# Top-k attention before a mixture of experts: pairs of heads with operands transposed on the host, v stationary

## The chip, the core and the metric

The kernel runs on one core of one Trainium2 chip. Time is device microseconds (us) of one launch. What the host does to the inputs ahead of the launch is not part of it. The engines that matter are TensorE (matmuls and transposes, shown as PE; its weight loads as PEld), VectorE (DVE), ScalarE (ACT), GpSimd (POOL) and the queue that issues most DMAs (SP).

## What is computed

Inputs q, k, v are (8, 8, 576, 64) in float32: 8 batches, 8 heads, 576 positions, 64 numbers a head. Per batch and head:

```
scores = q @ k.T / 8
kth    = 32nd largest of each row of scores
attn   = softmax(where(scores >= kth, scores, -1e9))
out    = attn @ v
```

The heads' outputs side by side make 4608 tokens of 512 numbers. Then a mixture of experts with 8 experts, each token going to one of them:

```
logits = x @ w_gate                    # (4608, 8)
e      = argmax(logits)                # one expert a token
gate   = softmax(logits)[e]
y      = gate * (relu(x @ w1[e]) @ w2[e])     # 512 -> 1024 -> 512
```

## The kernel before

Attention goes by pairs of batches p (four), and in a pair head by head (eight), so there are 32 units. The two batches' 2 x 576 queries of a head make nine tiles of 128 rows: four of the first batch, four of the second, and a ninth with both tails of 64. That is 288 tiles of 128 queries by 576 keys.

`load_head` brings q, k and v of a head with nine DMAs on SP, two heads ahead. `prep_head` turns q and k into qT and kT on TensorE (eight transposes of 128x128, two of 64 rows), with the first batch's 64 numbers on rows 0 to 63 and the second's on rows 64 to 127; ScalarE copies them from PSUM.

A tile then goes through three steps. `scores` (L183) multiplies one 64-row half of qT with kT, 512 keys and then 64, and ScalarE copies the 576 scores to s. `weights` (L194) finds the 32 largest on VectorE in four rounds of MAX8 with three MATCH_REPLACE between them; after the first round ScalarE makes nbias (L203) and the exponential ex (L204); then one instruction (L212) compares s with the 32nd value, multiplies by ex and sums the row into z. VectorE adds a small number to z and takes its reciprocal rz. `values` (L223) transposes the weights on TensorE into pm (four blocks) and pt (the last 64 keys), ScalarE copies them to wm and wt, and five products with wm and wt stationary and 64 columns of v streaming give 128 queries by 64 numbers; ScalarE scales them by rz into the token buffer x (L241). The result shares the PSUM buffer of pt, of which there is one.

The loop (L333) emits for tile n: the scores of tile n+1, the weights of tile n, the values of tile n-1. The order in which instructions stand on each engine is not that of the text: a planner orders them by when their operands and buffers should be ready; each engine then takes its own list in order. Buffers: two for scores in PSUM, three for s, two for ex and scr, three for w.

When a pair of batches is through, `route` (L243) computes the logits in nine rounds (four transposes into PSUM, a copy to xT, four products), the expert of each token and its place in that expert's list. GpSimd scatters the token ids to the lists with nine indirect DMAs, each of which waits for the one before; x goes to DRAM. A routing's logits share the one PSUM buffer of pt, its transposes the one of `prep_head`.

After the last routing, a table says which expert and which piece of its list each of 25 blocks of 256 tokens has. For each block, the expert's weights (4 MB) are loaded two blocks ahead, tokens are gathered, transposed, and put through both layers (L410, L417), and the rows are scattered to the output.

Of the kernel before, what the change touches and what calls it, by code (L numbers as in the profile page):

```python
# [30 lines left out]
def kernel(  # L31
    ctx: ExitStack,
    tc: tile.TileContext,
    q: bass.AP,
    k: bass.AP,
    v: bass.AP,
# [16 lines left out]
    B, H, S, D = q.shape  # L53
# [3 lines left out]
    P = 128  # L57
    NC = 4
    SM = NC * P
    ST = S - SM  # L60
    NT = 2 * NC + 1
# [9 lines left out]
    assert D == 64 and ST == 64 and Dm == H * D and N == B * S and B % 2 == 0  # L71
# [5 lines left out]
    wpool = ctx.enter_context(tc.tile_pool(name="wpool", bufs=3))  # L77
# [28 lines left out]
    for p in range(NP):  # L106
        t = const.tile([P, NT], I32, name=f"tok_id{p}")
        b0 = 2 * p * S
        nc.gpsimd.iota(t[:, 0:NC], pattern=[[1, NC]], base=b0, channel_multiplier=NC)
        nc.gpsimd.iota(t[:, NC:2 * NC], pattern=[[1, NC]], base=b0 + S, channel_multiplier=NC)  # L110
# [7 lines left out]
    def load_w(e):  # L118
        w1 = wpool.tile([P, 1, DT, F], F32, name="w1")
        nc.sync.dma_start(w1, w1v[:, bass.ds(e, 1), :, :])  # L120
        w2 = wpool.tile([P, 1, FT, Dm], F32, name="w2")
        nc.sync.dma_start(w2, w2v[:, bass.ds(e, 1), :, :])
        return w1, w2

    cnt = None
    first_w = None

    with (
        tc.tile_pool(name="pad", bufs=1) as padp,
        tc.tile_pool(name="load", bufs=2) as load,  # L130
        tc.tile_pool(name="att", bufs=2) as att,
        tc.tile_pool(name="xp", bufs=2) as xp,
# [5 lines left out]
        loaded, ready = {}, {}  # L138

        def load_head(p, h):  # L140
            got = []
            for nm, src in (("q", q), ("k", k), ("v", v)):
                if nm == "v":
                    m = load.tile([P, 2, NC, D], F32, name="v_m", bufs=3)
                    nc.sync.dma_start(
                        m, src[2 * p:2 * p + 2, h, 0:SM, :].rearrange("b (p c) d -> p b c d", c=NC)
                    )
                else:
                    m = load.tile([P, NC, 2, D], F32, name=nm + "_m", bufs=3)
                    for b in range(2):  # L150
                        nc.sync.dma_start(
                            m[:, :, b, :], src[2 * p + b, h, 0:SM, :].rearrange("(p c) d -> p c d", c=NC)
                        )
                t = load.tile([ST, 2, D], F32, name=nm + "_t", bufs=3)
                nc.sync.dma_start(t, src[2 * p:2 * p + 2, h, SM:S, :].rearrange("b p d -> p b d"))
                got.append((m, t))
            loaded[p, h] = got

        def prep_head(p, h):
            (qm, qt), (km, kt), vv = loaded.pop((p, h))  # L160
            xT = []
            for nm, m in (("qT", qm), ("kT", km)):
                o = att.tile([P, S], F32, name=nm)
                ps = ps_1.tile([P, SM], F32, name="tr")
                for c in range(NC):
                    nc.tensor.transpose(ps[:, c * P:(c + 1) * P], m[:, c, :, :], ident)
                nc.scalar.copy(o[:, 0:SM], ps)
                xT.append(o)
            ps = ps_1.tile([P, SM], F32, name="tr")
            for n, t in enumerate((qt, kt)):  # L170
                nc.tensor.transpose(ps[:, n * ST:(n + 1) * ST], t, ident[0:ST, 0:ST])
            for n in range(2):
                nc.scalar.copy(xT[n][:, SM:S], ps[:, n * ST:(n + 1) * ST])
            ready[p, h] = (xT[0], xT[1], vv)

        def parts(i):
            """(batch of the pair, rows of the tile, columns of its queries)"""
            if i < 2 * NC:
                b, c = divmod(i, NC)
                return [(b, slice(0, P), slice(c * P, (c + 1) * P))]  # L180
            return [(b, slice(b * ST, (b + 1) * ST), slice(SM, S)) for b in range(2)]

        def scores(p, h, i):  # L183
            qT, kT, _ = ready[p, h]
            ps = ps_s.tile([P, S], F32, name="sc")
# [4 lines left out]
            s = att.tile([P, S], F32, name="s", bufs=3)  # L190
            nc.scalar.copy(s, ps)  # L191
            return s

        def weights(s):  # L194
# [16 lines left out]
            z = small.tile([P, 1], F32, name="z")  # L211
            nc.vector.scalar_tensor_tensor(  # L212
                out=w, in0=s, scalar=tops[:, TOP_K // 8 - 1, 7:8], in1=ex,
                op0=ALU.is_ge, op1=ALU.mult, accum_out=z,
            )
            rz = small.tile([P, 1], F32, name="rz", bufs=4)
            nc.vector.tensor_scalar_add(z, z, EPS)
            nc.vector.reciprocal(rz, z)
            return w, rz

        xt = {}

        def values(p, h, i, w, rz):  # L223
            _, _, (vm, vt) = ready[p, h]
            if h == 0 and i == 0:
                xt[p] = xp.tile([P, NT, XW], F32, name="x")
            pm = ps_w.tile([P, NC, P], F32, name="wT")
            pt = ps_1.tile([P, 512], F32, name="po")
# [3 lines left out]
            wm = att.tile([P, NC, P], F32, name="wm")  # L232
            wt = att.tile([ST, P], F32, name="wt")
            nc.scalar.copy(wm, pm)  # L234
            nc.scalar.copy(wt, pt[0:ST, 0:P])  # L235
            po = pt[:, P:P + D]
            for b, rows, _ in parts(i):
                for c in range(NC):
                    nc.tensor.matmul(po[rows, :], wm[:, c, rows], vm[:, b, c, :], start=(c == 0), stop=False)  # L239
                nc.tensor.matmul(po[rows, :], wt[:, rows], vt[:, b, :], start=False, stop=True)  # L240
            nc.scalar.activation(xt[p][:, i, h * D:(h + 1) * D], po, AF.Copy, scale=rz)  # L241

        def route(p):  # L243
# [4 lines left out]
            for i in range(NT):  # L248
                ps = ps_1.tile([P, DT, P], F32, name="xtr", tag="tr")
# [55 lines left out]
            for b in range(2):  # L305
                r0 = (2 * p + b) * S
                nc.sync.dma_start(
                    x_rows[r0:r0 + SM, :].rearrange("(p c) w -> p c w", c=NC), x[:, b * NC:(b + 1) * NC, :]
# [3 lines left out]
        heads = [(p, h) for p in range(NP) for h in range(H)]  # L312
        work = [(p, h, i) for p, h in heads for i in range(NT)]
        load_head(*heads[0])
        load_head(*heads[1])
        prep_head(*heads[0])

# [7 lines left out]
        def finish(n, wr):  # L325
            p, h, i = work[n]
            values(p, h, i, *wr)
            if h == H - 1 and i == NT - 1:
                route(p)

        s_next = scores(*work[0])
        wr_prev = None
        for n, (p, h, i) in enumerate(work):  # L333
            hn = p * H + h
            if i == 0 and hn + 2 < len(heads):
                load_head(*heads[hn + 2])
            if i == NC and hn + 1 < len(heads):
                prep_head(*heads[hn + 1])
            if i == 0 and hn == 3:
                first_w = load_w(0)  # L340
            s = s_next
            if n + 1 < len(work):
                s_next = scores(*work[n + 1])
            wr = weights(s)
            if wr_prev is not None:
                finish(n - 1, wr_prev)
            wr_prev = wr
        finish(len(work) - 1, wr_prev)
# [23 lines left out]
    with (  # L372
        tc.tile_pool(name="mlp", bufs=2) as mlp,
# [6 lines left out]
        def load_slot(j):  # L380
# [5 lines left out]
            else:  # L386
                w = load_w(nc.sync.value_load(slot_i[0:1, 0, j:j + 1], min_val=0, max_val=E - 1))
# [71 lines left out]
```

## Time and profile before

| | |
|---|---|
| three runs | 2889.40, 2894.57, 2893.51 us; median 2893.51 |
| profiled execution, span from first to last instruction | 2891.7 us; no other time of that execution is given |
| TensorE busy | 2733.2 us (95%) |
| VectorE busy | 1743.3 us (60%) |
| ScalarE busy | 858.8 us (30%) |
| GpSimd busy | 138.4 us (5%) |

A profile row of a group gives line, engine, operation, output and inputs by the program's names, their shapes, the count, then busy time in us and the mean duration of one in ns, then the engine's idle time ahead of them and what ended it. A timeline row gives start and duration in us. Instructions of one engine overlap a little, so the distance from start to start, not the duration, is what one costs in a row of them. A float32 product has two records on TensorE.

### The profile page before, as it was taken

What the parts mean: (1) busy time and instruction counts of PE and PEld (TensorE: products, weight loads), DVE (VectorE), ACT (ScalarE), POOL (GpSimd) and SP (SyncE); (2) the same over time, 40 slices, a digit from 0 to 9 for tenths busy, and PEclk for the clock granted to TensorE, in tenths of its full rate; (3) what the DMA queues carried; (4) which work ended last, traced back from release to release, by engine and by line L of the source; (5) the groups of instructions that cost most, each with busy time, mean ns of one, the idle gap of its engine ahead of it and who ended that gap; (6) DMA issues with size and microseconds to landing.
All of it is one profiled execution on the core that took longest, in us unless ns stands there. A gap on an engine that the chain in (4) does not pass through costs nothing. (4 is left out here: it accounts for less than half of the span.)

```text
span 2891.7 us, 27400 instructions
## 1 busy us (share of the span) xinstructions
PE 2733.2 (95%) x9288; PEld 1798.0 (62%) x9288; DVE 1743.3 (60%) x4280; ACT 858.8 (30%) x2097; POOL 138.4 (5%) x165
## 2 busy tenths in 40 slices
PE   8999999999999989999999899999829999999999
PEld 5666666666666666666666566666626666666665
DVE  7888888588888857888885788889410101010100
ACT  3343343233333333333333333433300111111010
POOL 0000000000000000000000100000011111111110
PEclk9999999999999999999999999999999999999999
DMA  4000000100000010000000200000045545455540
GB/s 126 13 17 13 13 17 5 54 16 13 17 13 13 9 49 15 19 13 13 17 9 5 57 13 9 5 5 1 1 169 178 183 171 181 167 183 177 173 156 4
DMA packets 144669, 167.19 MB, mean 58 GB/s; under 512 B 90764, under 2 KB 99084, under 8 KB 143506
## 3 DMA queue, kind: packets, MB, share of 16 engines
q1 hardware_dynamic: 135378, 142.84, 15.7%
q0 software_dynamic: 9152, 22.60, 2.0%
q8 instruction: 74, 1.21, 0.2%
q14 instruction: 65, 0.53, 0.1%
HBM read 146.34 MB, written 22.73 MB: 58 GB/s over the span
## 5 line engine op out<-in xcount | busy, mean ns | idle before, releaser
L189 PE MATMUL sc<-kT,qT 64*128 64x64 f32 (+3 forms) x1280 | 802.1, 765 | 0.0
L239 PEld LDWEIGHTS po<-v_m,wm 128*128 128x128 f32 (+1 forms) x2560 | 515.1, 306 | 349.8 <-ACT ex L204 327.3
L201 DVE MAX8 tops<-scr 128x8 f32<-128x576 f32 x864 | 622.8, 748 | 0.0
L239 PE MATMUL po<-v_m,wm 128*128 128x64 f32 (+1 forms) x2560 | 573.6, 406 | 5.0 <-ACT wt L235 4.8
L206 DVE MATCH_REPLACE8 scr<-tops,scr 128x576 f32<-128x576 f32 x576 | 426.8, 743 | 0.0
L189 PEld LDWEIGHTS sc<-kT,qT 64*128 64x128 f32 (+1 forms) x1280 | 290.2, 293 | 190.0 <-issue 153.2
L201 DVE MAX8 tops<-s 128x8 f32<-128x576 f32 x288 | 218.0, 757 | 309.0 <-ACT s L191 307.3
L410 PE MATMUL ph<-xTs,w 128*128 128x256 f32 x1600 | 353.0, 381 | 14.1 <-DVE xTs L405 14.1
L417 PE MATMUL py<-w,hT 128*128 128x512 f32 x800 | 347.4, 592 | 0.0
L241 ACT ACTIVATE x<-po,rz 128x64 f32<-128x64 f32 x288 | 90.7, 315 | 861.5 <-PE po L240 722.1
L410 PEld LDWEIGHTS ph<-xTs,w 128*128 128x128 f32 x1600 | 302.8, 191 | 60.1 <-DVE xTs L405 19.8
L230 PE MATMUL wT<-ident,w 128*128 128x128 f32 x1152 | 319.7, 430 | 0.0
L421 DVE TENSOR_SCALAR y<-py,xg 128x512 f32<-128x512 f32 x50 | 37.6, 751 | 447.4 <-PE py L417 447.4
L413 ACT ACTIVATE hT<-ph 128x256 f32<-128x256 f32 x200 | 76.8, 384 | 696.4 <-PE ph L410 637.7
L417 PEld LDWEIGHTS py<-w,hT 128*128 128x128 f32 x800 | 152.0, 190 | 180.7 <-issue 179.4
L212 DVE SCALAR_TENSOR_TENSOR w<-s,tops,ex 128x576 f32<-128x576 f32 x288 | 231.7, 805 | 13.6 <-PE po L231 9.2
L230 PEld LDWEIGHTS wT<-ident,w 128*128 128x128 f32 x1152 | 213.2, 219 | 28.3
L204 ACT ACTIVATE ex<-s,nbias 128x576 f32<-128x576 f32 x288 | 223.0, 774 | 8.4
L234 ACT COPY wm<-wT 128x512 f32<-128x512 f32 x288 | 168.8, 586 | 175.5 <-PE wT L230 166.9
L206 DVE MATCH_REPLACE8 scr<-tops,s 128x576 f32<-128x576 f32 x288 | 213.9, 743 | 0.0
L240 PE MATMUL po<-v_t,wt 64*128 64x64 f32 (+1 forms) x640 | 206.0, 424 | 0.0
L191 ACT COPY s<-sc 128x576 f32<-128x576 f32 x288 | 182.0, 632 | 6.3 <-PE sc L189 3.9
(92 smaller groups left out, 1313.2 us busy)
## 6 DMA issues: line engine op xcount, KB each, us to landing
w<-in_moe_w_dram SPq DMA_DIRECT2D x50, 2048.0 KB, 9.9
x_rows<-x SPq DMA_DIRECT2D x8, 1026.0 KB, 6.1
q_m<-in_q_dram SPq DMA_DIRECT2D x64, 128.0 KB, 2.6
k_m<-in_k_dram SPq DMA_DIRECT2D x64, 128.0 KB, 2.5
v_m<-in_v_dram SPq DMA_DIRECT2D x32, 256.0 KB, 2.9
x_rows<-x SPq DMA_DIRECT2D x8, 128.2 KB, 5.5
q_t<-in_q_dram SPq DMA_DIRECT2D x32, 32.0 KB, 2.2
k_t<-in_k_dram SPq DMA_DIRECT2D x32, 32.0 KB
```

The lines of the kernel that those rows point to most:

```text
L189: nc.tensor.matmul(ps[rows, c0:c1], qT[d, cols], kT[d, c0:c1], start=True, stop=True)
L191: nc.scalar.copy(s, ps)
L201: nc.vector.max(out=tops[:, r, :], in_=src)
L204: nc.scalar.activation(ex, s, AF.Exp, scale=scale, bias=nbias)
L206: nc.vector.match_replace(out=scr, in_to_replace=tops[:, r, :], in_values=src, imm_value=NEG)
L212: nc.vector.scalar_tensor_tensor(out=w, in0=s, scalar=tops[:, TOP_K // 8 - 1, 7:8], in1=ex, op0=ALU.is_ge, op1=ALU.mult, accum_out=z,)
L230: nc.tensor.transpose(pm[:, c, :], w[:, c * P:(c + 1) * P], ident)
L234: nc.scalar.copy(wm, pm)
L239: nc.tensor.matmul(po[rows, :], wm[:, c, rows], vm[:, b, c, :], start=(c == 0), stop=False)
L240: nc.tensor.matmul(po[rows, :], wt[:, rows], vt[:, b, :], start=False, stop=True)
L410: nc.tensor.matmul(ph, w1[:, 0, dt, f * P:(f + 1) * P], xT[:, dt, :], start=(dt == 0), stop=(dt == DT - 1))
L417: nc.tensor.matmul(py, hT[:, f, c * P:(c + 1) * P], w2[:, 0, f, :], start=(f == 0), stop=(f == FT - 1))
```

## The change

Attention now goes batch by batch and by pairs of heads: (b, u) with u from 0 to 3, 32 units as before. q and k come from the host as (8, 512, 576), already transposed, so that two heads lie on the two 64-row halves of a 128-row slice; v comes as (8, 576, 512). `load_head` and `prep_head` are gone; `load_qk` loads two units at a time, `load_v` a whole batch.

A unit's nine tiles are four of the first head, four of the second, and the ninth with both heads' last 64 queries. `scores` takes a pair of tiles, one of each head on the same queries, and emits their products alternately, each as two times 288 keys; a score tile has two PSUM banks. `weights` makes nbias on GpSimd and leaves z as one column of a unit's (128, 9). `transposed` copies the transposed weights of all nine tiles into one large buffer wT (and wTt for the last 64 keys). `outputs`, once a unit, multiplies with v stationary (64 columns of a head) and the weights streaming, 288 queries at a time, the two heads into the two halves of one PSUM tile; copies the result to oT; transposes it back; and multiplies by the reciprocals on VectorE on the way into x. Routing's transposes share the PSUM buffer of the weights' tail, its logits that of the outputs. There are four buffers for s. The experts' weight pool is opened after attention; the first expert's weights have a pool of their own and are asked for in the fifth unit (before, the fourth). The numbering of tokens in tiles, and with it the row stores, changes.

```diff
+        def load_qk(b, u):
+            qb = load.tile([P, 2, S], F32, name="qb")
+            nc.sync.dma_start(qb, qt[b, u * P:(u + 2) * P, :].rearrange("(u p) s -> p u s", p=P))
...
-            for b, rows, cols in parts(i):
-                d = slice(b * D, (b + 1) * D)
-                for c0, c1 in ((0, SM), (SM, S)):
-                    nc.tensor.matmul(ps[rows, c0:c1], qT[d, cols], kT[d, c0:c1], start=True, stop=True)
+            for i in tiles:
+                ps = ps_s.tile([P, 2, SM], F32, name="sc")
+                todo += [(ps, h, rows, cols) for h, rows, cols in parts(i)]
+                got.append(ps)
+            for j in range(2):
+                for ps, h, rows, cols in todo:
+                    d = slice(h * D, (h + 1) * D)
+                    nc.tensor.matmul(
+                        ps[rows, j, 0:HF], qu[d, cols], ku[d, j * HF:(j + 1) * HF], start=True, stop=True
+                    )
+            out_s = []
+            for ps in got:
+                s = att.tile([P, 2, HF], F32, name="s", bufs=4)
+                nc.scalar.copy(s, ps[:, :, 0:HF])
...
-                    nc.scalar.mul(nbias, tops[:, 0, 0:1], -scale)
+                    nc.gpsimd.tensor_scalar(nbias, tops[:, 0, 0:1], -scale, None, ALU.mult)
...
-            nc.vector.tensor_scalar_add(z, z, EPS)
-            nc.vector.reciprocal(rz, z)
...
+        def transposed(b, u, i, w):
+            wT, wTt, _ = units[b, u]
+            pm = ps_w.tile([P, NC, P], F32, name="wTm")
+            pt = ps_1.tile([P, SM], F32, name="wTl")
             for c in range(NC):
                 nc.tensor.transpose(pm[:, c, :], w[:, c * P:(c + 1) * P], ident)
             nc.tensor.transpose(pt[0:ST, 0:P], w[:, SM:S], ident)
...
+                nc.scalar.copy(wT[:, :, h, q], pm)
+                nc.scalar.copy(wTt[:, h, q], pt[0:ST, 0:P])
...
+        def outputs(b, u):
+            vb = vs_of[b]
+            wT, wTt, z = units[b, u]
+            rz = small.tile([P, NT + 1], F32, name="rz", bufs=2)
+            nc.vector.tensor_scalar_add(rz[:, 0:NT], z, EPS)
+            nc.vector.reciprocal(rz[:, 0:NT], rz[:, 0:NT])
+            nc.vector.tensor_copy(rz[0:ST, NT:NT + 1], rz[ST:P, 2 * NC:NT])
+            oT = att.tile([P, S], F32, name="oT")
+            for j in range(2):
+                q = slice(j * HF, (j + 1) * HF)
+                po = ps_1.tile([P, SM], F32, name="po")
+                for c in range(KC):
+                    for h in range(2):
+                        rows = slice(h * D, (h + 1) * D)
+                        vs = slice(u * P + h * D, u * P + (h + 1) * D)
+                        if c < NC:
+                            lhsT, rhs = vb[:, c, vs], wT[:, c, h, q]
+                        else:
+                            lhsT, rhs = vb[0:ST, c, vs], wTt[:, h, q]
+                        nc.tensor.matmul(po[rows, 0:HF], lhsT, rhs, start=(c == 0), stop=(c == KC - 1))
+                nc.scalar.copy(oT[:, q], po[:, 0:HF])
...
+            px = ps_1.tile([P, SM], F32, name="px", tag="po")
+            for t in range(NC):
+                nc.tensor.transpose(px[:, t * P:(t + 1) * P], oT[:, t * P:(t + 1) * P], ident)
+            nc.vector.tensor_tensor(
+                x[:, half * NC:(half + 1) * NC, u * P:(u + 1) * P].rearrange("p t (h d) -> p t h d", h=2),
+                px[:, :].rearrange("p (t h d) -> p t h d", t=NC, h=2),
+                _inner(rz[:, 0:2 * NC].rearrange("p (t h) -> p t h", h=2), D), op=ALU.mult,
+            )
+            pl = ps_1.tile([P, SM], F32, name="pl", tag="po")
...
-                ps = ps_1.tile([P, DT, P], F32, name="xtr", tag="tr")
+                ps = ps_1.tile([P, DT, P], F32, name="xtr", tag="wTl")
...
+        groups = [(i, NC + i) for i in range(NC)] + [(2 * NC,)]
+        work = [(b, u, g) for b in range(B) for u in range(U) for g in groups]
...
+            s_now = s_next
             if n + 1 < len(work):
                 s_next = scores(*work[n + 1])
+            for i, s in zip(g, s_now):
+                w = weights(b, u, i, s)
+                if last is not None:
+                    finish(*last)
+                last = (b, u, i, w)
```

`finish` calls `transposed`; after a unit's ninth tile it calls `outputs`, and after the fourth unit of every second batch `route`.

## Rows read from the trace of the kernel before

**Rows 1.** The page, part 1: busy us, share of the span, instructions.

```profile
PE 2733.2 (95%) x9288; PEld 1798.0 (62%) x9288; DVE 1743.3 (60%) x4280; ACT 858.8 (30%) x2097; POOL 138.4 (5%) x165
```

**Rows 2.** Windows: length, busy us of PE, PEld, DVE, ACT, POOL; clock, DMA share, GB/s.

```profile
0.00:12.20 12.20, 5.48 (x15) 3.24 (x16) 0.80 (x6) 3.42 (x6) 3.83 (x29) 1.00 0.55 124
12.20:2062.40 2050.20, 1976.74 (x6536) 1289.08 (x6535) 1662.91 (x4105) 772.05 (x1877) 26.49 (x27) 1.00 0.07 19
2062.40:2155.30 92.90, 34.05 (x151) 28.95 (x151) 9.36 (x50) 6.48 (x14) 12.47 (x13) 1.00 0.22 75
2155.30:2891.70 736.40, 716.92 (x2590) 476.70 (x2588) 70.24 (x121) 76.83 (x200) 95.60 (x96) 1.00 0.46 162
```

**Rows 3.** Timeline of PE, one steady tile: start us, duration us, what.

```profile
1003.64 0.63 PE L189 MATMUL sc<-kT,qT 64*128 64x64 f32 x2
1004.20 1.11 PE L230 MATMUL wT<-ident,w 128*128 128x128 f32 x4
1005.11 0.42 PE L231 MATMUL po<-ident,w 128*64 128x128 f32 x1
1005.46 2.07 PE L189 MATMUL sc<-kT,qT 64*128 64x512 f32 x2
1007.46 1.97 PE L239 MATMUL po<-v_m,wm 128*128 128x64 f32 x8
...
1009.84 0.42 PE L189 MATMUL sc<-kT,qT 64*128 64x64 f32 x1
```

**Rows 4.** Timeline of DVE, from one MAX8 on s to the next.

```profile
956.61 0.76 DVE L201 MAX8 tops<-s 128x8 f32<-128x576 f32 x1 [1.09 <-ACT s L191]
...
962.91 0.13 DVE L217 TENSOR_SCALAR z<-z 128x1 f32<-128x1 f32 x1
962.97 0.75 DVE L201 MAX8 tops<-s 128x8 f32<-128x576 f32 x1
```

**Rows 5.** Groups of instructions by line and shape, all of the span.

```profile
L410 PE MATMUL ph<-xTs,w 128*128 128x256 f32 x1600 | 353.0, 381 | 14.1 <-DVE xTs L405 14.1
...
L212 DVE SCALAR_TENSOR_TENSOR w<-s,tops,ex 128x576 f32<-128x576 f32 x288 | 231.7, 805 | 13.6 <-PE po L231 9.2 <-ACT ex L204 4.3
...
L234 ACT COPY wm<-wT 128x512 f32<-128x512 f32 x288 | 168.8, 586 | 175.5 <-PE wT L230 166.9 <-PE po L239 7.0
...
L235 ACT COPY wt<-po 64x128 f32<-64x128 f32 x288 | 74.3, 258 | 57.0 <-PE po L231 56.6 <-PE wT L230 0.3
...
L405 DVE COPY xTs<-xtp 128x512 f32<-128x512 f32 x50 | 32.2, 682 | 9.9 <-PE xtp L404 9.9
...
L263 DVE TENSOR_TENSOR oh<-lgs,mx 128x72 f32<-128x72 f32 x4 | 0.9, 224 | 0.0
```

**Rows 6.** Timeline of PE at the start: scores of four tiles alone.

```profile
9.16 8.74 PE L189 MATMUL sc<-kT,qT 64*128 64x512 f32 x16
```

**Rows 7.** Timeline of PE: products on the two 64-row halves.

```profile
974.18 0.47 PE L240 MATMUL po<-v_t,wt 64*128 64x64 f32 x1
974.19 0.47 PE L189 MATMUL sc<-kT,qT 64*128 64x64 f32 x1
```

**Rows 8.** Timeline during the second routing (first row) and the last.

```profile
1060.67 0.23 DVE L259 COPY lgs<-lg 128x72 f32<-128x72 f32 x1 [27.32 <-PE lg L255]
...
2071.70 5.29 PE L255 MATMUL lg<-wg,xT 128*128 128x8 f32 x24 [0.40 <-ACT x L241]
...
2092.82 1.88 PE L255 MATMUL lg<-wg,xT 128*128 128x8 f32 x8 [0.73 <-ACT xT L253]
...
2096.37 1.88 PE L255 MATMUL lg<-wg,xT 128*128 128x8 f32 x8 [0.73 <-ACT xT L253]
```

**Rows 9.** Waits: who waited for whom, us in total, times, longest.

```profile
POOL lists L294 <- DMA lists<-tok_id,posi: 97.5, 32, 6.2
```

**Rows 10.** TensorE's longest pause (window, columns as Rows 2) and its first work afterwards.

```profile
2101.00:2151.00 50.00, 0.12 (x1) 0.00 (x0) 5.62 (x34) 0.00 (x0) 12.47 (x13) 1.00 0.32 105
...
2151.45 1.08 PE L404 MATMUL xtp<-ident,xg 128*128 128x128 f32 x4 [50.33 <-DMA xg<-x_rows,src]
```

More of the change, by code (lines that the diff above doesn't have):

```diff
@@ L52 @@
     nc = tc.nc
-    B, H, S, D = q.shape
+    B, HD, S = qt.shape
     N, Dm = out.shape
@@ L57 @@
     P = 128
+    D = 64
+    U = HD // P
     NC = 4
@@ L70 @@
     LIST = E * N
-    assert D == 64 and ST == 64 and Dm == H * D and N == B * S and B % 2 == 0
+    assert ST == 64 and Dm == HD and N == B * S and B % 2 == 0
     assert N % BLK == 0 and LIST % P == 0 and TOP_K == 32 and Dm == 512
@@ L116, with load_w @@
     w2v = moe_w2.rearrange("e (ft p) d -> p e ft d", p=P)
-    def load_w(e):
-        w1 = wpool.tile([P, 1, DT, F], F32, name="w1")
+    def load_w(pool, e):
+        w1 = pool.tile([P, 1, DT, F], F32, name="w1")
         nc.sync.dma_start(w1, w1v[:, bass.ds(e, 1), :, :])
-        w2 = wpool.tile([P, 1, FT, Dm], F32, name="w2")
+        w2 = pool.tile([P, 1, FT, Dm], F32, name="w2")
         nc.sync.dma_start(w2, w2v[:, bass.ds(e, 1), :, :])
@@ L137 @@
     ):
[L138 to L171, printed above, removed]
-            for n in range(2):
-                nc.scalar.copy(xT[n][:, SM:S], ps[:, n * ST:(n + 1) * ST])
-            ready[p, h] = (xT[0], xT[1], vv)
+        qk, vs_of, xt, units = {}, {}, {}, {}
@@ L194, in weights, with scores @@
-        def weights(s):
+                h, c = divmod(i, NC)
+                return [(h, slice(0, P), slice(c * P, (c + 1) * P))]
+            return [(h, slice(h * ST, (h + 1) * ST), slice(SM, S)) for h in range(2)]
+        def scores(b, u, tiles):
+            qu, ku = qk[b, u]
+            todo = []
+            got = []
+            for i in tiles:
[12 more added lines that the diff above has]
+                nc.scalar.copy(s, ps[:, :, 0:HF])
+                out_s.append(s)
+            return out_s
@@ L195, in weights @@
+        def weights(b, u, i, s3):
+            s = s3[:, :, :].rearrange("p j k -> p (j k)")
             tops = small.tile([P, TOP_K // 8, 8], F32, name="tops")
@@ L210, in weights @@
             w = att.tile([P, S], F32, name="w", bufs=3)
-            z = small.tile([P, 1], F32, name="z")
+            z = units[b, u][2]
+            c = 2 * NC if i == 2 * NC else 2 * (i % NC) + i // NC
             nc.vector.scalar_tensor_tensor(
                 out=w, in0=s, scalar=tops[:, TOP_K // 8 - 1, 7:8], in1=ex,
-                op0=ALU.is_ge, op1=ALU.mult, accum_out=z,
+                op0=ALU.is_ge, op1=ALU.mult, accum_out=z[:, c:c + 1],
             )
-            rz = small.tile([P, 1], F32, name="rz", bufs=4)
-            nc.vector.tensor_scalar_add(z, z, EPS)
-            nc.vector.reciprocal(rz, z)
[L219 to L228, printed above, removed]
+            return w
+        def transposed(b, u, i, w):
+            wT, wTt, _ = units[b, u]
+            pm = ps_w.tile([P, NC, P], F32, name="wTm")
+            pt = ps_1.tile([P, SM], F32, name="wTl")
             for c in range(NC):
@@ L231, in values @@
             nc.tensor.transpose(pt[0:ST, 0:P], w[:, SM:S], ident)
[L232 to L240, printed above, removed]
@@ L307, in route @@
                 nc.sync.dma_start(
-                    x_rows[r0:r0 + SM, :].rearrange("(p c) w -> p c w", c=NC), x[:, b * NC:(b + 1) * NC, :]
+                    x_rows[r0:r0 + SM, :].rearrange("(c p) w -> p c w", p=P), x[:, b * NC:(b + 1) * NC, :]
                 )
                 nc.sync.dma_start(x_rows[r0 + SM:r0 + S, :], x[b * ST:(b + 1) * ST, 2 * NC, :])
[L312 to L316, printed above, removed]
+        load_qk(0, 0)
+        load_v(0)
         pad = padp.tile([P, LIST // P], I32, name="pad")
@@ L323, with finish @@
         nc.sync.dma_start(x_rows[N:N + 1, :], zrow)
[L325 to L329, printed above, removed]
-        s_next = scores(*work[0])
[L332 to L341, printed above, removed]
+        groups = [(i, NC + i) for i in range(NC)] + [(2 * NC,)]
+        work = [(b, u, g) for b in range(B) for u in range(U) for g in groups]
+        def finish(b, u, i, w):
+            transposed(b, u, i, w)
+            if i == 2 * NC:
+                outputs(b, u)
+                if u == U - 1 and b % 2 == 1:
+                    route(b // 2)
+        s_next = scores(*work[0])
+        last = None
+        for n, (b, u, g) in enumerate(work):
+            if g == groups[0]:
+                units[b, u] = (
+                    wtp.tile([P, NC, 2, S], F32, name="wT"),
+                    wtp.tile([ST, 2, S], F32, name="wTt"),
+                    small.tile([P, NT], F32, name="z", bufs=2),
+                )
+                if u % 2 == 0:
+                    b2, u2 = (b, u + 2) if u + 2 < U else (b + 1, 0)
+                    if b2 < B:
+                        load_qk(b2, u2)
+                        if u2 == 0:
+                            load_v(b2)
+                if (b, u) == (1, 0):
+                    first_w = load_w(firstp, 0)
+            s_now = s_next
             if n + 1 < len(work):
                 s_next = scores(*work[n + 1])
[L344 to L348, printed above, removed]
+            for i, s in zip(g, s_now):
[3 more added lines that the diff above has]
+                last = (b, u, i, w)
+        finish(*last)
         nb = small.tile([1, E], F32, name="nb", bufs=1)
@@ L431, with _laid_out @@
             block(*ahead.pop(0))
-_INS = ['q', 'k', 'v', 'moe_w_gate', 'moe_w1', 'moe_w2']
 _OUTS = [((4608, 512), 'float32')]
+def _laid_out(inputs):
+    import numpy as _np
+    q, k, v = (_np.asarray(inputs[n]) for n in "qkv")
+    B, H, S, D = q.shape
+    return {
+        "qt": q.transpose(0, 1, 3, 2).reshape(B, H * D, S),
+        "kt": k.transpose(0, 1, 3, 2).reshape(B, H * D, S),
+        "vt": v.transpose(0, 2, 1, 3).reshape(B, S, H * D),
+        "moe_w_gate": inputs["moe_w_gate"],
+        "moe_w1": inputs["moe_w1"],
+        "moe_w2": inputs["moe_w2"],
+    }
 def kernel(**inputs):
@@ L446 @@
     arrays, args = {}, []
-    for name in _INS:
-        a = _np.ascontiguousarray(inputs[name])
+    for name, a in _laid_out(inputs).items():
+        a = _np.ascontiguousarray(a)
         arrays[f"in_{name}_dram"] = a
```

52 lines of the change are left out of this document (35 added, 17 removed).

## The prediction

> **What bounds the kernel now.** I read the busy shares first, then cut the span into stretches, then read the order of time on TensorE and on VectorE inside one stretch, then the groups by shape. TensorE is busy 95% of the span and VectorE 60% [rows 1], but the shares mix two stages. The stretches [rows 2] part them: 12.2 us of start, 2050.2 us of attention, 92.9 us of turnover (last routing, lists, first gather), 736.4 us of experts. In attention TensorE is busy 1976.7 of 2050.2 us and VectorE 1662.9, so the second engine is only a fifth behind. One steady tile [rows 3] shows what TensorE does in 6.20 us without a gap: scores 2.0 + 0.56, transposes of the weights 1.26, and 2.38 for weights times v (1007.46 to 1009.84). 288 tiles of 6.20 are 1786 us; the rest is the making of qT and kT and the routing.
> VectorE's own floor is in [rows 4]: from one MAX8 on s to the next, without a gap, 6.36 us hold five MAX8 (0.66 by their starts), three MATCH_REPLACE (0.72 with their loads), one product and the two one-column ops. A tile has four MAX8, so it costs 6.36 - 0.66 = 5.70 us, and 288 of them 1642 us, the bulk of the 1662.9. What a lighter TensorE can give is therefore bounded: VectorE stands 2050.2 - 1662.9 = 387 us behind it.
>
> **TensorE after the change,** by units of nine tiles (32 of them).
> Scores: 576 key columns a tile as before, now as 2 x 288 on one 64-row half. Sixteen records, four tiles, took 8.74 us [rows 6]: 2.19 us a tile, 3.8 ns a column. So 19.7 us a unit if the halves take turns, 9.9 if the two heads' halves run together. That halves can run together is in [rows 7]: a product on rows 0 to 63 and a score on rows 64 to 127 start 0.01 us apart and both take 0.47 us. But the two score tiles of a pair come free only as two copies to s go, and each copy waits for the product of another tile, some 5.7 us apart; the planner issues what is ready. I take the serial 19.7 and keep 9.9 as the lower end.
> Weight transposes stay: 1.26 us a tile [rows 3], 11.3 a unit.
> Weights times v: 9 x 2.38 = 21.4 us go. In come 20 products of 288 columns with v stationary on 64 columns of the array. No row of before has that shape with a long moving side. At the expert's rate (353.0 us over 1600 records of 256 columns [rows 5], two records a product, 1.72 ns a column) one takes 0.50 us; at the half-array rate of [rows 6] 1.09. With the two heads in turn or together that is 5.0 to 21.8 us a unit. I take 10.9: half-array rate, heads together as in [rows 7].
> The Trainium skill's page "TensorEngine Tiling (Array Packing)", sections Overview and Performance Considerations, lets a streaming side of 64 be made stationary and two column tiles run at once, for up to twice the speed. No row here shows two column halves at once; by the page the term is 10.9 or 5.0, without it 21.8 or 9.9.
> Five transposes back cost 5 x 0.21 = 1.1; some ten changes of array shape at 0.14 (starts 0.35 apart instead of 0.21 in [rows 3]) 1.4. Sum 19.7 + 11.3 + 10.9 + 1.1 + 1.4 = 44.4 us a unit, ends 27 and 55. The 32 makings of qT and kT leave TensorE and ScalarE altogether.
>
> **VectorE after the change.** The add and the reciprocal per tile go: by its start the add holds the engine 0.06 us [rows 4], the reciprocal as long; 0.12 x 288 = 35 us (by twice the add's 0.13 us duration 75). Each unit adds a multiply of 128x512 out of PSUM: between the copy of that size, 0.682, and the product of 128x576, 0.805 [rows 5], say 0.75; one of 128 columns on 64 rows, between 0.22 of 72 columns and 0.68 of 512, say 0.3; and three ops on at most nine columns, at most 0.22 each, the time of the 72-column one [rows 5], 0.66. That is 1.7 x 32 = 55 us. 1662.9 - 35 + 55 = 1683 us, 52.6 a unit. This is more than TensorE's 44.4: VectorE becomes the bound, and TensorE's cuts below 52.6 are worth nothing.
>
> **What stands idle on VectorE then.**
> Start: the host's transposes spare the first chain; the first score needs two loads of 576 KB. I take 9.2 us for 12.2; ends 8 and 13.
> Routing: before, VectorE stood 27.3 us behind the logits [rows 8]. Routing now shares its PSUM buffer with the tails of the weight transposes. Nine rounds of 3.55 us (2092.82 to 2096.37 [rows 8]) are 32 us, after an output chain of about 12; w has three buffers, so VectorE gets some 3.9 tiles, 22 us, done meanwhile. 44 - 22 = 22 us, three times: 66. Ends 0 (routing fits into TensorE's slack) and 82 (as before).
> Unit ends: the multiply out of PSUM waits for transposes 1.26, copies 0.59 + 0.26 [rows 5], two rounds of ten products with a copy 2 x (5.45 + 0.5), transposes back 1.1: about 15 us. The first round needs no late tile and can run early. What queues behind the multiply on VectorE is the next tiles' search, and behind that their weights and transposes. The planner mixes rounds of two tiles [rows 4], so it has other work to put first. I take 2 us a unit, 64 us; ends 0 and 15.
> nbias moves from ScalarE to GpSimd, which takes in order: during routing it queues behind scatters that wait for each other's landing, 97.5 us in 32 waits [rows 9]. The exponential is wanted only at the product, at least three MAX8 and three replacements or 4.1 us after the MAX8 that feeds nbias, and more where two tiles mix; one such wait is 3.05 us. Without that cover, a quarter of 97.5, 24 us a routing. Taken at 0.
> Loads (q, k, v in larger pieces, still on SP), the first expert's weights issued later and from a pool of their own, and row stores in smaller pieces lie beside 2000 us of attention with DMA engines 7% busy [rows 2]: 0. The expert weights' pool opens where attention's buffers lay; those are free when slot 1's weights are asked for, late in the turnover, after nine scatters. If not, up to 10 us.
> Turnover: before, 92.9. The output chain is longer (about 12 us for 9, from 2062.4 [rows 2] to 2071.7 [rows 8]), and routing, which before took 26.6 us from there on (2071.70 to the end of the row at 2096.37) with rounds done ahead, takes nine rounds, 32. Together +8: 101. Experts unchanged, 736.4.
>
> **Sum.** 9.2 + 1683 + 66 + 64 + 101 + 736.4 = 2660 us, 8% less than the span of 2891.7. No time beside the span is given for the profiled execution; the median of the runs, 2893.5, is 1.8 above it, so I leave the sum as it is.
>
> **Rivals.**
> All unit ends covered: VectorE runs without a stop but for the routing. 2660 - 64 = 2596. For it: the two-tile mixing, w's three buffers, s's four. Against: engines take in order, and before, VectorE waited 27 us at one instruction [rows 8].
> TensorE remains the bound: heads never overlap, so a unit costs 19.7 + 11.3 + 21.8 + 2.5 = 55.3 us, with in-order waits say 57.6; 32 x 57.6 = 1843 for 1683 + 64: 2755. For it: no row shows two 64-column halves at once, and the score halves come ready apart. Against: [rows 7].
> Slower: the multiply out of PSUM stands on VectorE directly behind its unit's last product, and the whole chain of 15 us is exposed at each unit end: 2596 + 32 x 15 = 3076. It decides from (2891.7 - 2596)/32 = 9.2 us a unit on. Against it: a ready tile is there to be mixed in, as in [rows 4].
> The clock: TensorE will stand idle part of each unit. Before, it was idle for 50 us and the granted clock stayed 1.00, the 2.4 GHz level, and the first transposes after it took 1.08 us for four, as in the steady tile's 1.11 [rows 3, 10]. If pauses did bring it to 1.2 GHz, a unit would cost 2 x 44.4 us: 32 x 88.8 + 66 + 9 + 101 + 736 = 3754.
> That pauses bring the lower clock is what the Trainium skill says ("TensorE: Matmul & The Clock Gate", section Part 1); the rows of this case don't agree with it.
>
> **How the numbers follow.** Forecast 0.52 (2610 to 2720 around 2660), all covered 0.20, TensorE bound 0.20, slower by exposed chains 0.05, slower by the clock 0.01, gain lost to no change 0.02 over small mishaps. The range cuts the far halves of the two neighbours: 2555 to 2775. No change means within 0.2%, 6 us, about what runs of this kernel can tell. Faster 0.92, same 0.02, slower 0.06.
>
> **What would show it.** VectorE busy above 90% between the routings, 5.6 to 5.8 us a tile; TensorE near 80%; no group for qT or kT; twenty products a unit of about 1.1 us, two of them starting together. Gaps on VectorE before the multiply out of PSUM price the unit ends; one of 20 us before the logits, three times, the routing. The forecast is wrong if TensorE still has no gap in attention, if those waits pass 9 us a unit, if its clock falls, or if the experts' 736 us move.

## The result: 2673 us, and the profile after

The changed kernel takes 2673.37 us (median of 4 runs, 2672.9 to 2674.61) against 2893.56 (4 runs, 2889.4 to 2894.57): ratio 0.9242, 95% interval 0.9229 to 0.9255, 220 us less. The forecast was 2660.

The page of the changed kernel: the span; each engine's busy us, share and instructions; then the busy tenths and the granted clock in forty slices.

```profile
span 2671.2 us, 22208 instructions
PE 2038.4 (76%) x7208; PEld 1205.5 (45%) x7208; DVE 1736.8 (65%) x3864; ACT 718.1 (27%) x1457; POOL 199.7 (7%) x453
...
PE   5766677666776876677686677676199999999998
...
DVE  8999999699999869999986999995100010010000
...
PEclk8666656566656655655666656665599999999999
```

TensorE fell from 95% to 76% [rows 1]. In attention VectorE is full but for three dips (the routings), and the granted clock reads 0.5 to 0.7 (its records begin at 36.6 us) where the page before showed 1.00. The same stretches as [rows 2], with the same columns, then one unit without a routing:

```profile
0.00:10.10 10.10, 2.29 (x9) 1.28 (x9) 0.81 (x7) 1.98 (x3) 3.80 (x29) 1.00 0.79 251
10.10:1837.50 1827.40, 1285.50 (x4458) 701.24 (x4458) 1655.18 (x3686) 632.62 (x1242) 87.95 (x315) 0.62 0.07 21
1837.50:1934.00 96.50, 32.93 (x154) 25.76 (x155) 10.61 (x53) 6.68 (x13) 12.54 (x13) 0.54 0.24 71
1934.00:2671.20 737.20, 717.65 (x2590) 477.23 (x2588) 70.21 (x121) 76.83 (x200) 95.37 (x96) 1.00 0.45 162
752.30:807.00 54.70, 41.53 (x133) 21.56 (x132) 51.55 (x114) 19.22 (x38) 1.87 (x9) 0.56 0.06 22
```

All of the gain is in attention: 1827.4 us for 2050.2. VectorE is busy there for 1655.2, within 8 us of before, but idle for 172 in place of 387. In the unit, TensorE has 13 us to spare and VectorE 3.15. The waits of the whole kernel (us in total, times, longest) say where VectorE stands:

```profile
DVE x L262 <- PE px L261: 120.3, 31, 11.8
...
DVE lgs L291 <- PE lg L287: 78.1, 4, 26.4
```

Without the last unit's 6.6 and the last routing's 26.4, which fall into the turnover, 113.7 and 51.7 us lie inside attention: 165.4 of the 172. The timeline at a unit's end shows the first of them (start, duration, engine, line, work; in brackets the idle time ahead of it):

```profile
799.25 2.29 PE L182 MATMUL sc<-kb,qb 64*128 64x288 f32 x4
801.47 3.68 PE L253 MATMUL po<-wT,vb 128*64 128x288 f32 x16
805.08 0.70 PE L253 MATMUL po<-wTt,vb 64*64 64x288 f32 x4
805.83 0.40 ACT L254 COPY oT<-po 128x288 f32<-128x288 f32 x1 [5.26 <-PE po L253]
806.28 0.66 PE L261 MATMUL px<-ident,oT 128*128 128x128 f32 x4 [0.50 <-ACT oT L254]
806.97 0.69 DVE L262 TENSOR_TENSOR x<-px,rz 128x512 f32<-128x512 f32 x1 [3.04 <-PE px L261]
```

The second half of the unit's outputs, ten products in twenty records, takes 4.3 us, a copy and four transposes follow, and VectorE stands 3.04 us at the multiply out of PSUM. It does so once a unit: 2.5 to 3.6 us in 27 units, and 9.7 to 11.8 in the three in which a routing runs beside.

### The profile page after: what moved, and what is told of

Its sections match the earlier page's. It is cut to its first block, busy times and chain, and to the rows that moved or that the text cites. A ratio compares the mean times of both kernels' runs of the same rounds, so it can differ in the third digit from the quotient of the medians.

```text
span 2671.2 us, 22208 instructions
## 1 busy us (share of the span) xinstructions
PE 2038.4 (76%) x7208; PEld 1205.5 (45%) x7208; DVE 1736.8 (65%) x3864; ACT 718.1 (27%) x1457; POOL 199.7 (7%) x453
## 5 line engine op out<-in xcount | busy, mean ns | idle before, releaser
L223 PE MATMUL wTm<-ident,w 128*128 128x128 f32 x1152 | 282.1, 392 | 490.1 <-DVE w L212 473.2
L182 PE MATMUL sc<-kb,qb 64*128 64x288 f32 (+1 forms) x1280 | 575.2, 654 | 33.1 <-ACT s L188 26.0
L223 PEld LDWEIGHTS wTm<-ident,w 128*128 128x128 f32 x1152 | 187.7, 198 | 667.3 <-issue 498.9
L182 PEld LDWEIGHTS sc<-kb,qb 64*128 64x128 f32 (+1 forms) x1280 | 279.2, 269 | 205.4 <-issue 109.7
L253 PE MATMUL po<-wT,vb 128*64 128x288 f32 x1024 | 277.5, 642 | 1.4 <-ACT wT L228 0.9
L203 ACT ACTIVATE ex<-s,nbias 128x576 f32<-128x576 f32 x288 | 223.8, 777 | 94.0 <-POOL nbias L202 93.7
L228 ACT COPY wT<-wTm 128x512 f32<-128x512 f32 x256 | 150.1, 586 | 171.3 <-PE wTm L223 168.1
L202 POOL TENSOR_SCALAR nbias<-tops 128x1 f32<-128x1 f32 x288 | 60.8, 211 | 1664.3 <-DVE tops L200 1393.5
L253 PEld LDWEIGHTS po<-wT,vb 128*64 128x64 f32 x1024 | 108.6, 213 | 163.4 <-issue 157.5
```

Source lines behind the costliest of these rows:

```text
L182: nc.tensor.matmul(ps[rows, j, 0:HF], qu[d, cols], ku[d, j * HF:(j + 1) * HF], start=True, stop=True)
L223: nc.tensor.transpose(pm[:, c, :], w[:, c * P:(c + 1) * P], ident)
L228: nc.scalar.copy(wT[:, :, h, q], pm)
L253: nc.tensor.matmul(po[rows, 0:HF], lhsT, rhs, start=(c == 0), stop=(c == KC - 1))
```

## The clock that the rows of before did not show

The prediction took 1.00 in [rows 2, 10] for a measurement. In that trace the first record of TensorE's clock lies at 2157.6 us, and the page shows 1.00 where there is none. The pace of a known operation fills the gap. Four 128x128 transposes of the changed kernel, in two windows (clock is the third column from the end) and in TensorE's timeline:

```profile
1823.00:1825.00 2.00, 1.30 (x5) 0.88 (x5) 2.00 (x6) 0.61 (x2) 0.21 (x1) 0.50 0.00 0
1829.00:1831.00 2.00, 1.87 (x9) 0.72 (x8) 2.00 (x6) 0.83 (x3) 0.21 (x1) 1.00 0.00 0
```

```profile
1823.27 1.09 PE L223 MATMUL wTm<-ident,w 128*128 128x128 f32 x4 [3.31 <-DVE w L212]
...
1825.03 3.89 PE L253 MATMUL po<-wT,vb 128*64 128x288 f32 x14 [0.46 <-ACT wT L228]
...
1829.48 0.66 PE L223 MATMUL wTm<-ident,w 128*128 128x128 f32 x4
```

At granted 0.50 (1.2 GHz) they take 1.09 us, at 1.00 (2.4 GHz) 0.66. Before, the steady tile's took 1.11 [rows 3], and in the whole attention of before no two neighbouring ones start less than 0.213 us apart (856 pairs; in the changed kernel down to 0.109): it ran at 1.2 GHz, with TensorE 96% busy. The times agree: the seven runs of the kernel before beside the first experiments took 2889.05 to 2896.52 us, and those whose traces give a mean clock of 0.64 to 0.66 are not slower than those that give 1.00. The first work after TensorE's pause ran at 1.2 GHz as well, 1.08 [rows 10]; the changed kernel's, after the same pause in the turnover, is recorded at 0.50:

```profile
1849.00:1934.00 85.00, 22.96 (x96) 19.55 (x97) 9.07 (x46) 4.04 (x8) 12.54 (x13) 0.50 0.28 81
1934.00:1937.80 3.80, 3.80 (x11) 3.07 (x10) 0.86 (x2) 0.10 (x1) 0.07 (x1) 0.50 1.05 392
1938.00:1945.00 7.00, 7.00 (x35) 6.15 (x34) 0.00 (x0) 1.49 (x5) 1.61 (x2) 1.00 1.03 395
```

```profile
1929.88 1.09 PE L446 MATMUL xtp<-ident,xg 128*128 128x128 f32 x4 [54.50 <-DMA xg<-x_rows,src]
```

The experts begin at 0.50 and read 1.00 from 1937.8 us on, TensorE having been busy without a gap since 1934.0; in attention the clock rose within a run of output products (at 1828.6) and fell again among transposes, scores and gaps.

## The experiments

My theory: before, TensorE at 1.2 GHz set the pace of attention; the change lightens it until VectorE does, and 165 us of waits remain at unit ends and routings. Rivals: one of the two edits (the host's transposes, v stationary) does it all; VectorE was the bound before too; the clock matters little. No run has v stationary alone, or the change without its other buffers and loads, so what is not the host's transposes stays one piece.

**The host's transposes alone.** In the kernel before, qT and kT come by DMA already turned; v keeps its place.

```diff
-            for nm, src in (("q", q), ("k", k), ("v", v)):
+            for nm, src in (("q", q), ("k", k)):
+                m = load.tile([P, S], F32, name=nm + "_T", bufs=3)
+                nc.sync.dma_start(m, src[p, h])
...
-                    nc.tensor.transpose(ps[:, c * P:(c + 1) * P], m[:, c, :, :], ident)
...
+            qT, kT, vv = loaded.pop((p, h))
```

> The kernel before with q and k alone transposed on the host; nothing else changed. Theory (TensorE bounds attention before): what leaves TensorE leaves the time: ten transposes and their waits, about 3.3 us a head, 32 heads, 105 us: 2785 us. Rival (the making of qT and kT lay beside other work): within 20 us of 2893. Second rival: the copies on ScalarE counted too, 150 us or more: 2740.

Measured 2805.72 us, ratio 0.9696 (0.9679 to 0.9714): 90 us less than the kernel before beside it (2895.72), where the theory had 105: two fifths of the change's gain, so this edit alone is not all of it. The first clock record of its trace lies at 383.3 us: 1.00 for 10.2 us, then 0.50 from 393.5 to 2069. Two windows, ahead of the records and at 0.50, and TensorE's timeline in the first, in the 10 us at 1.00, and in the second:

```profile
100.00:300.00 200.00, 199.59 (x648) 132.43 (x647) 181.26 (x445) 76.69 (x191) 0.00 (x0) 1.00 0.06 17
1500.00:1700.00 200.00, 190.69 (x609) 121.89 (x609) 163.00 (x416) 72.23 (x172) 8.81 (x9) 0.50 0.09 26
```

```profile
202.55 1.11 PE L221 MATMUL wT<-ident,w 128*128 128x128 f32 x4
...
385.11 0.66 PE L221 MATMUL wT<-ident,w 128*128 128x128 f32 x4
...
1501.39 1.06 PE L221 MATMUL wT<-ident,w 128*128 128x128 f32 x4
...
1505.08 2.39 PE L180 MATMUL sc<-k_T,q_T 64*128 64x512 f32 x4
```

The pace is one and the same with 1.00 shown and with 0.50 recorded, at 95% and more of busy time; with 1.00 recorded it is another.

**A search of three rounds in place of four, before and after.** It takes the same work from VectorE in both kernels (the weights keep 24 keys of a row and not 32).

```diff
+ROUNDS = 3
...
-            for r in range(TOP_K // 8):
+            for r in range(ROUNDS):
```

> The kernel before with three rounds of the search in place of four (the 24 largest are kept, so this part of the computation is changed): one MAX8 and one MATCH_REPLACE a tile less, 1.38 us of VectorE, 397 us over 288 tiles. Theory (TensorE bounds attention): the time stays within 30 us of 2893. Rival (VectorE has a share in the bound through in-order waits): 100 us or more are gained.

> The changed kernel with three rounds of the search in place of four (the 24 largest are kept). Theory (VectorE is the bound now): nearly all of 397 us goes, 2280 to 2340 us. Rival (a chain through TensorE and ScalarE sets the unit's 54.6 us): 2550 us or more.

Attention's window of the kernel before, then of the changed one, each with the short search:

```profile
12.30:2028.00 2015.70, 1949.42 (x6533) 1280.47 (x6531) 1270.90 (x3241) 768.20 (x1877) 27.13 (x27) 0.67 0.08 20
```

```profile
10.30:1362.90 1352.60, 1130.10 (x4458) 620.08 (x4458) 1254.60 (x2822) 616.69 (x1242) 113.13 (x315) 0.70 0.09 28
```

Before: 392 us less work on VectorE bought 32.5, a little more than the 30 allowed (2863.18, two runs, ratio 0.9894, 0.9872 to 0.9915), and TensorE stayed 97% busy; it was the bound. After: 400 us less work bought 475 (2198.82, ratio 0.7601, 0.7587 to 0.7616). VectorE is the bound now. The 74 us on top, which I had not expected, are waits at the multiply that went with it (113.7 to 26.7 us in attention). The attention's mean clock is higher here, 0.70 for 0.62, and VectorE's list is in another order: in 25 of the 32 units three to eight search instructions (MAX8, MATCH_REPLACE) stand between the last product and the multiply, where in the changed kernel it mostly follows a product at once. How much is due to which I did not try.

**Unread products, to hold the clock.** Ahead of each tile's scores TensorE gets products that nobody reads: before, three of 448 columns a tile; after, six of 224. They only add work to TensorE; the score tile of before grows from 576 to 1024 columns to hold them, which no run tries by itself.

```diff
+            ps = ps_s.tile([P, 2 * SM], F32, name="sc")
+            for _ in range(3):
+                nc.tensor.matmul(ps[:, S:2 * SM], ident, kT[:, 0:2 * SM - S], start=True, stop=True)
...
+                for k in range(6):
+                    nc.tensor.matmul(ps[:, k % 2, HF:SM], ident, ku[:, 0:SM - HF], start=True, stop=True)
```

> The kernel before with three products more per tile that nobody reads: 128 rows, 448 columns streaming, into unused PSUM columns ahead of the scores. Theory (TensorE ran attention at 1.2 GHz, although the profile shows 1.00 where it has no record: 128-column transposes start 0.21 us apart there, 0.13 in stretches of the changed kernel granted 1.00): the filler lifts the clock, a tile costs 6.2/2 + 3 x 0.77 = 5.4 us, less than VectorE's 5.7, and the time falls to 2600 to 2720 us although TensorE does more. Rival (the clock was full already): 288 x 3 x 0.77 = 665 us are added, 3555 us. Third case (low clock, not lifted): 288 x 3 x 1.5, 1300 us are added, 4190 us.

> The changed kernel with six products more per tile that nobody reads (128 rows, 224 columns, into unused PSUM columns ahead of the scores). Theory (what is left of VectorE's idle time comes from TensorE's low clock: outputs and routing run at it): the waits before the multiply out of PSUM fall from 114 us to about 30, those before the logits from 52 to 40, the turnover by 10: 2570 to 2600 us. Rival (VectorE is the bound and the filler stands ahead of the outputs in TensorE's order): 2673 to 2750.

The kernel before with them: attention's window, and TensorE's timeline in one tile.

```profile
16.40:1844.70 1828.30, 1781.89 (x8267) 1082.52 (x8266) 1650.79 (x4105) 775.83 (x1879) 26.11 (x27) 0.97 0.09 21
```

```profile
199.24 1.77 PE L187 MATMUL sc<-kT,ident 128*128 128x448 f32 x4
200.94 1.29 PE L191 MATMUL sc<-kT,qT 64*128 64x512 f32 x4
202.17 0.66 PE L232 MATMUL wT<-ident,w 128*128 128x128 f32 x4
```

2670.77 us (2662.75 to 2676.03; ratio 0.922, 0.9195 to 0.9244): the time of the change, without the change, and with 864 products more. The clock is 0.97, one tile's scores (four records) take 1.29 us for the 2.39 of the first experiment, the transposes 0.66 for 1.11. Why these products lift the clock and the kernel's own, at 95% busy, do not, no run here shows. The changed kernel with them takes 2584.72 (ratio 0.8945, 0.8905 to 0.8985), 89 less than without; its attention and its waits at the multiply:

```profile
15.90:1745.50 1729.60, 1527.60 (x7890) 1120.15 (x7890) 1655.28 (x3686) 640.94 (x1242) 88.45 (x315) 0.96 0.07 21
```

```profile
DVE x L264 <- PE px L263: 38.0, 11, 7.9
```

VectorE's own work is the same to 0.1 us, and two thirds of the unit-end waits are gone. That is the low clock only in part for certain, since VectorE's list is in another order too, often with two or more search instructions ahead of the multiply. But in 12 units the multiply still follows a product at once, as in the changed kernel, and waits for nothing. One of them, from VectorE's timeline:

```profile
179.31 0.80 DVE L214 SCALAR_TENSOR_TENSOR w<-s,tops,ex 128x576 f32<-128x576 f32 x1
...
180.03 0.69 DVE L264 TENSOR_TENSOR x<-px,rz 128x512 f32<-128x512 f32 x1
```

**Host's transposes and unread products,** v not stationary: the two edits above together in the kernel before.

```diff
+            qT, kT, vv = loaded.pop((p, h))
...
+            for _ in range(3):
+                nc.tensor.matmul(ps[:, S:2 * SM], ident, kT[:, 0:2 * SM - S], start=True, stop=True)
```

> The kernel before with q and k transposed on the host and the three unread products per tile; v streams as before. Theory (the change's gain is VectorE's relief from a TensorE at 1.2 GHz, and any way to that is worth the same): the filler alone gave 2671; without the makings of qT and kT VectorE waits less for s, 119 us to about 50: 2590 to 2620 us, below the changed kernel's 2673 without any v stationary. Rival (v stationary is needed for the rest): 2660 or more.

2598.57 us (ratio 0.8971, 0.8951 to 0.8991), 75 less than the changed kernel; attention 1752.5 with VectorE busy 1652.6. With the clock held, pairs of heads with v stationary bring it to 2584.72, 14 us, and the two intervals overlap. This speaks for it that in the change they brought mainly less work for a slow TensorE; with v stationary alone not run, it is not shown.

**Outputs two tiles later.** The outputs of a unit are put behind the weight transposes of the second tile after its last one.

```diff
+LATE = 2
...
             if i == 2 * NC:
-                outputs(b, u)
-                if u == U - 1 and b % 2 == 1:
-                    route(b // 2)
+                due.append([LATE, b, u])
...
+            while due and due[0][0] <= 0:
+                release()
```

> The changed kernel with a unit's outputs emitted two tiles later, so that the multiplies out of PSUM rank behind the next tiles' search. Theory (VectorE stands at that multiply because it takes in order and has other work): the 114 us of waits nearly vanish, 2560 to 2590 us. Rival (the planner puts the multiply where its operands should be ready, whatever the emission): 2660 to 2680.

2611.97 us (ratio 0.9028, 0.9008 to 0.9047), 61 less than the changed kernel: less than expected. The wait at the first multiply is gone from attention (the 7.7 is the last unit's, in the turnover), but a new one stands at the second, which takes the last 64 queries; its transpose shares the one PSUM buffer with the first multiply's and starts only once that has read it:

```profile
DVE lgs L292 <- PE lg L288: 79.5, 4, 25.6
...
DVE x L270 <- PE pl L269: 25.0, 11, 5.9
...
DVE x L263 <- PE px L262: 7.7, 1, 7.7
```

**The routing spread as well.** Its nine rounds are issued two by two, one pair behind each tile.

```diff
+                if i % 2 == 1:
+                    yield
...
+            for g in list(going):
+                if next(g, going) is going:
+                    going.remove(g)
...
-                route(b // 2)
+                going.append(route(b // 2))
```

> As the run with later outputs, and the nine rounds of routing emitted two at a time, one pair after each tile of the next unit. Theory (a routing costs 27 us over a plain unit because its rounds hold the buffer of the weights' tails): three routings give back 20 to 25 us each beside the outputs' 100: 2490 to 2530 us. Rival (the rounds' own chain of copies and products delays the tiles wherever they stand): within 15 us of the run with later outputs.

2591.13 us (ratio 0.8947, 0.8932 to 0.8962), 21 less than the last one and well short of what I expected. The waits for the logits inside attention only fell to 38.3 us (64.7 less the last 26.4), and the first multiply got 17.4 back:

```profile
DVE lgs L295 <- PE lg L288: 64.7, 4, 26.4
...
DVE x L263 <- PE px L262: 17.4, 4, 6.9
```

Moving the issue of the rounds did not take the wait away; why VectorE still comes to the logits early I did not settle. With everything together, below, it is gone.

**nbias on ScalarE again.**

```diff
-                    nc.gpsimd.tensor_scalar(nbias, tops[:, 0, 0:1], -scale, None, ALU.mult)
+                    nc.scalar.mul(nbias, tops[:, 0, 0:1], -scale)
```

> The changed kernel with nbias back on ScalarE. Theory (its place costs nothing, the exponential is wanted far later): 2665 to 2680 us. Rival (ScalarE's 94 us of waits for nbias behind GpSimd's scatters reach VectorE): 20 us or more are gained.

2663.68 us (ratio 0.9196, 0.9181 to 0.9211): 10 less. The changed kernel's row is the first; the waits at the multiply with nbias on ScalarE, the second.

```profile
ACT ex L203 <- POOL nbias L202: 93.7, 73, 7.8
```

```profile
DVE x L262 <- PE px L261: 106.0, 32, 6.6
```

ScalarE stood 93.7 us behind GpSimd, nearly all of it hidden from the product: VectorE waits only 0.9 us for the exponential. Without it the waits at the multiply are 14 us less (120.3 to 106.0). The difference lies in the three units in which a routing runs, 31.5 us together in the changed kernel and 11.4 here; the others' rose by 6. The first of them, in the changed kernel (three rows) and with nbias on ScalarE (the last):

```profile
525.35 0.77 ACT L203 ACTIVATE ex<-s,nbias 128x576 f32<-128x576 f32 x1 [4.88 <-POOL nbias L202]
...
526.55 0.59 ACT L231 COPY wT<-wTm 128x512 f32<-128x512 f32 x1
...
534.17 0.69 DVE L262 TENSOR_TENSOR x<-px,rz 128x512 f32<-128x512 f32 x1 [9.68 <-PE px L261]
```

```profile
530.54 0.69 DVE L262 TENSOR_TENSOR x<-px,rz 128x512 f32<-128x512 f32 x1 [3.69 <-PE px L261]
```

ScalarE waits 4.88 us for an nbias that GpSimd makes between two scatters, and the copy of the unit's last weights, which the outputs need, stands behind that exponential in its list.

**All together:** later outputs, spread routing, nbias on ScalarE, unread products; then with two unread products a tile.

```diff
+                for k in range(6):
...
-                for k in range(6):
+                for k in range(2):
```

> The changed kernel with later outputs, routing spread, nbias on ScalarE and six unread products per tile. Theory (VectorE's own 1647 us of attention is the floor; start 10, turnover 100, experts 736: 2493): idle time falls from 93 (routing spread) and 88 (filler) to about 40: 2530 to 2550 us. Rival (both cures touch the same waits, and the filler delays the scores): 2575 to 2590.

> As all together, with two unread products per tile in place of six. Theory (what counts is whether the clock stays up): if two hold it, 2530 us or a little less, since TensorE is freer; if they don't, the granted clock falls back to about 0.75 and the time to 2570 to 2590.

Attention's window with six, then with two:

```profile
16.60:1689.20 1672.60, 1470.35 (x7890) 1090.98 (x7890) 1653.04 (x3686) 679.13 (x1530) 27.38 (x27) 0.96 0.08 22
```

```profile
14.00:1715.50 1701.50, 1281.58 (x5602) 806.60 (x5602) 1652.67 (x3686) 675.33 (x1531) 26.93 (x27) 0.79 0.08 22
```

With six: 2528.3 us (2526.44 to 2531.52; ratio 0.8729, 0.871 to 0.8747), the fastest of all and faster than both kernels. VectorE idles 20 us in attention (1672.6 less 1653.0); what is left there is its own work, most of it the search. Its waits for the logits are down to the last routing's, in the turnover:

```profile
DVE lgs L297 <- PE lg L290: 25.8, 1, 25.8
```

Whether the clock or the order did that is not separated.

With two: 2554.51 (ratio 0.8813, 0.8787 to 0.8838), between the two cases expected, and the attention's mean clock is 0.79: two don't hold it all the way.

## Why the prediction was right, and which step failed

The time is 13 us from the forecast, and the mechanism is the one forecast: TensorE drops below VectorE, which then sets attention. The terms, predicted and measured on the span: start 9.2 and 10.1; VectorE's work 1683 and 1655.2; waits 66 + 64 = 130 and 172; turnover 101 and 96.5; experts 736.4 and 737.2. So 0.9 - 27.8 + 42 - 4.5 + 0.8 is 11 us more than 2660: two errors of opposite sign cover each other, and that is luck.

VectorE's work. The tile came to 5.56 us (two tiles between the MAX8 below, from VectorE's timeline), 5.58 by the forecast's terms (5.70 less 0.12); the unit's additions to 1.47 (multiplies 0.692 and 0.276, small ops 0.50), 1.7 forecast. That is 6 + 7 us of the 28; the other 15 lie in what I had put beside the tiles (the 1662.9 less the 1642), where 7 us are left of 21.

```profile
819.88 0.75 DVE L200 MAX8 tops<-s 128x8 f32<-128x576 f32 x1
...
831.00 0.76 DVE L200 MAX8 tops<-s 128x8 f32<-128x576 f32 x1
```

The terms of the waits that were mis-sized: unit ends, 2 us each, are 2.5 to 3.6, and 9.7 to 11.8 in the three units with a routing. The routing's wait for the logits is 17 us each, 22 forecast. The late outputs show that the unit ends are a matter of the order of issue, beside the clock: put two tiles later, all of the first multiply's wait inside attention goes. The mixing of two tiles did not cover it of itself. The nbias term, taken at 0, is 10 us: I looked only at the product that needs the exponential, not at the copies that stand behind it on ScalarE.

TensorE's unit is 41.5 us, 44.4 forecast. Scores cost 2.29 us a tile (four records, at 799.25 above), 2.19 forecast with the halves in turn; and the two heads' outputs do run together: sixteen records, four pairs of products, in 3.68 us are 0.92 a pair, 1.09 forecast (granted 0.50 up to 804.6 us). At 1.00 a pair takes 0.54 (last row of this text), where the expert's rate would make it 0.99 in turn. At this point the trace agrees with the Trainium skill's page "TensorEngine Tiling (Array Packing)", section Overview, on independent tiles and up to twice the speed, which no row of before could show.

The step that failed is the reading of the clock. "Half-array rate" [rows 6] is for the most part no property of 64 rows: it is the 1.2 GHz level, as one tile's scores show, 1.29 against 2.39 us (1.29 is 2.2 ns a column, still above the expert's 1.72). And [rows 10] did not show a TensorE that keeps 2.4 GHz through a pause, but one that was at 1.2 GHz before and after it. The sum survived by luck: every row of attention that it used already carried the low clock, so 44.4 us a unit is a price at 1.2 GHz. By the prediction's own sign ("if its clock falls") nothing fell: it had been low all along. For the same reason the clock rival was wrong: it doubled rows that were already slow. I called the rule that a TensorE with pauses comes to the lower clock ("TensorE: Matmul & The Clock Gate", section Part 1, in the Trainium skill) unsupported by this case; the changed kernel's rows agree with it, 0.50 after the 54.5 us pause and 1.00 only from 3.8 us into the experts, and so does the mean of 0.62 in attention; but pauses are not all of it, as the first experiment's 0.50 at 95% busy shows. Nor was a TensorE below VectorE's 52.6 us a unit "worth nothing" to speed up: with the clock held the changed kernel took 89 us less.

The bound by TensorE (2755) and the exposed chain (3076) were rightly put aside: TensorE has 13 us of slack a unit, and 3 us of the 15 are exposed. All unit ends covered (2596) is what outputs two tiles later come near to: 2611.97.

## What to carry to other kernels

Before a trace's clock is used, compare the pace of one known operation in that stretch with a stretch where the clock is recorded; a row without a record is no evidence of full speed, and a TensorE that is 96% busy can still run at half of it. To find the bound, take the same work from one engine in both kernels: what that buys (32 us for 392 before, 475 for 400 after) says it more plainly than busy shares. When the second engine becomes the bound, look at once for the instruction at which it waits in order, and move the work that feeds it ahead or that instruction back.

## What the hardware did that I had not expected

Adding work to TensorE made the kernel before faster by 225 us (2895.72 to 2670.77). The granted clock stayed at 0.50 through stretches of 95% busy time (1500 to 1700 us of the first experiment), and 864 products of 448 columns that nobody reads held it at 0.97. Products with 64 stationary columns of the two heads run two at a time: a pair takes 3.68 / 4 = 0.92 us in the changed kernel, and in the best version, at the higher clock, 2.16 / 4 = 0.54, from the row below of its timeline.

```profile
803.90 2.16 PE L256 MATMUL po<-wT,vb 128*64 128x288 f32 x16
```
